# Attention and two feed-forward layers on one core: pinned first splits, four bias buffers, later loads and a new order of the attention stage

## The chip, the core and the metric

The kernel runs on one core of one Trainium2 chip. TensorE (PE) multiplies matrices from SBUF into PSUM, VectorE (DVE) and ScalarE (ACT) work elementwise and read PSUM, GpSimd (POOL) works elementwise on SBUF alone, and SyncE (SP) issues nearly all DMAs, each in its own queue and in order. The metric is device time in microseconds (us); lower is better.

## The reference

```
scores = q @ k.T / sqrt(D)                       # B=2, H=8, S=576, D=64
x      = log1p(|i - j|) / log1p(max(i, 1))
bias   = relu(x * w1 + b1) @ w2                  # hidden width 32, one value for each head
attn   = softmax(scores + bias);  y = attn @ v   # then tokens x 512
out1   = sum_e p[:, e] * (relu(y @ W1[e]) @ W2[e])        # 4 experts, 512 -> 1024 -> 512
h      = out1 @ w_in;   P = a0+a1*h+a2*h^2+a3*h^3;   Q = 1+|b0||h|+|b1|h^2
out    = (P / (Q + 1e-6)) @ w_out                # 512 -> 2048 -> 512
```

All of it is float32. Where a product runs in the faster float32r form, its operand is split into a high part and a remainder, and the two parts are multiplied apart.

## The kernel before

Three stages follow each other: attention, which ends at about 197 us of the span, the expert layer, and the second feed-forward layer. The change touches only the attention stage.

**The bias.** The 576 x 576 bias of the eight heads is made in 36 groups `gg` of 16 query rows. For each group four tiles `hid` are made (`hidden`, L443 on ACT or L445 on DVE: one add and one relu over 288 to 576 columns, SBUF to SBUF), the PE multiplies them by a 32-column weight into one bank (`products`, L460), and one engine scales the bank into a row buffer `bo` (`combine`, L477 on ACT or L479 on DVE: two instructions for the first 32 groups, one for the last four). Each filled row of `bo` is stored to DRAM (`store`, L466), and after eight groups a chunk of bias for the first pair of heads is read back (`load_bias`, L543). There are two buffers `bo` of four rows each, in the pool slots that weights use later.

**One pass of attention.** Eight passes `n` take two heads each. Raw `q`, `k`, `v` are loaded (`load_raw`); `q` and `k` are split into a high part (`split_hi`, L584 on ACT, L586 on POOL) and a remainder (`split_lo`, L592 on POOL or DVE), transposed by the PE (`qk_T`, L608) and copied out on ACT (L616); `kl` is a copy of `kh` with its halves swapped, made by two DMAs (L621, L622). Nine groups `g` of 128 rows of scores follow (`scores`, L651). For each, DVE adds the bias and finds the row's extreme (`biased`, L665), ACT takes the exponential (`exps`, L673), DVE makes the reciprocal of the sums (L679, L684), DVE or POOL scales the rows (`norm`, L694), the PE transposes them (`transp`, L711; `transp_rest`, L724 and L727), and ACT or DVE copies them out (`copies`, L737 and L739). Twice a pass `av` multiplies them by the values: one matmul of all 128 value columns for the tile `pe` that the two heads share (L750), then four pairs of 64-column matmuls, one for each head (L753).

**What sets the order.** Nothing loops in this order in the program. `attention` gives every step as an operation with an engine, a duration, a list of steps that it needs and an urgency; `Flow.emit` plays these operations through, one engine each, and issues them in the order of the starts that come out. `PICK` says which engine takes each step that several could do, `CFG` holds the urgencies, `LAG`, `START` and `ARRIVES` the assumed delays. On the chip each engine then works its queue strictly in that order, and waits on semaphores. The planner lets steps of POOL and some of DVE (`PORT`: the tiles `hid`, `norm`, `split_lo`) not overlap; nothing in the built program enforces this. `TURN` is what the planner charges the PE for a change between array shapes of 32, 64 and 128 columns.

Of the kernel before, what the change touches and what calls it, by code (L numbers as in the profile page):

```python
# [9 lines left out]
F32 = mybir.dt.float32  # L10
# [14 lines left out]
P = 128  # L25
# [3 lines left out]
def f32_of_bits(b):  # L29
# [15 lines left out]
START = dict(PE=7.0, ACT=6.0, DVE=5.9, POOL=6.0, SP=7.5)  # L45
ARRIVES = dict(k=7.5, q=8.5, v=12.0, ident=6.5, ltab=10.0)
# [3 lines left out]
PICK = dict(hid="DDDDADAAADADDDADDADDAADDDDAAADDADDADDAADADDDDDDADDDDDDDDADDDDDADDDDDADDA"  # L50
              "DADADDDADDADDDADADDDAADADADDDDDDADDDADDADADDADDDADDAADDDDDDDADAAAADDDDDD",
            comb="AADDAAADDAADAAADADDAAADAAAADAAAAADDD",
            norm="DPDDPPDPPDPDDDPPDPDDDPDPDPPPPPPDPDPPDDDPDDPDPDDPPPDPPPPDPPPDDDPDDPPDPDPD",
            copy="ADADAADAAADDDAADDADDADDADADAADADAADAADDDADDAAAAADADADAADADDAAADDAADADDAA",
            rest="AAAAAAAADAAADAAAAAAAADAAAAAAAADAAAAAAAADAAAADAAAAAAADAAAAAAAADDAAADAAADD",
            high="PPAPAAPAPAAAAPPP",
            low="PPPDPPPDPDDPPPDP")

LAG = {"PE": .2, "ACT": .16, "DVE": .17, "POOL": .14, "SP": 4.2, "": 0.0, "own": .1, "ownPE": 0.0}
CFG = dict(S=(727.25, 1885.1, -835.03, -1091.88), R=(-435.51, -579.68, 887.76, 715.99),  # L60
           E=(2212.38, 3581.84, 2714.22, 1346.79), A=(-3009.34, -17.34, -2741.04, 809.11),
           N=(-1089.85, -18.23, -1346.32, 1155.82), T=(-970.49, -103.24, -1026.56, -1581.52),
           H=(-626.93, 112.8, -71.3, -1255.47), L=(1318.56, -792.88, -3831.2, -2180.55),
           V=(1383.81, 1813.71, 2683.79, -2574.27), G=(-1937.23, -222.49, -2871.65, -240.27),
           X=(-271.21, -1565.23, -1071.66, 1882.08), sk=(2779.05, -696.25, 887.14, 2612.94),
           sq=(-733.34, 2450.48, 615.97, 34.95), sv=(108.87, 720.22, 1146.45, -407.83),
           qk=(-1735.11, 1178.98, -1793.42, 1880.39), qq=(-2386.03, 493.54, -2804.99, -1502.57),
           kl=(-555.07, -2633.95, 1999.51, 3316.56), b=(1465.24, -1009.62, -3395.64, 567.95), NPB=5, EPS=0.0,
           w0=58, w1=24, w2=56, rk=(2354.82, 1606.83, 519.78, 448.01), rq=(678.94, -1446.52, 1914.62, -188.04),
           rv=(1641.63, 2113.44, -124.18, -2095.68), st=-137.14, F=1386.21,  # L70
           b0=(-2989.02, -989.69, -701.83, -1532.45, -694.41), b1=(659.94, -3385.72, 1251.53, -536.4, 233.82),
           b2=(-3325.06, -1303.49, -2104.11, -2246.44, -1403.66),
           b3=(-3088.15, -311.99, 937.07, 2166.6, 909.33), b4=(-2727.97, -2702.25, -1351.83, 1603.0, -344.56))


class Flow:
    def __init__(self, eps, **busy):
        self.ops, self.free, self.caps, self.eps = [], {"": 0.0, "port": 0.0, **busy}, {}, eps
        self.mode = 128
# [33 lines left out]
    def emit(self):  # L113
# [7 lines left out]
        while ready:  # L121
# [6 lines left out]
            start, _, _, o = min((c for c in cand if first[c[3]["eng"]] == now and c[0] <= now + self.eps), key=lambda c: c[1:3])  # L128
# [30 lines left out]
class Kernel:  # L159
    def __init__(self, ctx, tc, t):  # L160
        self.ctx, self.tc, self.nc, self.t = ctx, tc, tc.nc, t


# [236 lines left out]
    def bias_setup(self):  # L400
# [17 lines left out]
        self.load_raw(0, "v")  # L418
# [19 lines left out]
        def hidden(gg, q, e):  # L438
            tt = 4 * gg + q
            ht = hid[gg, q] = hids[:, tt % 12, 0:width(gg)]  # L440
            d, c = dtab[:, 0:width(gg)] if gg < NM else ltab[:, 572 - 4 * tt:572 - 4 * tt + S], shift[:, tt:tt + 1]
            if e == "ACT":
                nc.scalar.activation(out=ht, in_=d, func=AF.Relu, bias=c)  # L443
            else:
                nc.vector.tensor_scalar(out=ht, in0=d, scalar1=c, scalar2=0.0, op0=ALU.add, op1=ALU.max)  # L445
# [25 lines left out]
        def combine(gg, e):  # L471
# [8 lines left out]
            if G == 0:  # L480
                outs[b] = self.wpool.tile([P, 4, S + MARGIN * (gg < NM)], F32, tag="we", bufs=2, name="bo")
# [13 lines left out]
        def bias_ops(fl, biasop):  # L495
# [3 lines left out]
            for gg in range(NG):  # L499
# [6 lines left out]
                if gg % 4 == 0:  # L506
                    bo = fl.hold("bo", 2)
                co = fl.pick("comb", gg, {"ACT": .8 if gg < NM else .75, "DVE": .87 if gg < NM else .7}, u("b2"), lambda e, gg=gg: combine(gg, e), [po, co], take=[bo] if gg % 4 == 0 else [], free=[ph])
                stored.append(co if gg >= NM else fl.op("SP", .5, u("b3"), lambda gg=gg: store(gg), [co], free=[bo] if gg % 4 == 3 else []))
                if gg % 8 == 7:  # L510
                    biasop[0, c] = fl.op("SP", .6, u("b4"), lambda c=c: self.load_bias(0, c), stored)
                    stored = []
            biasop[0, 4] = fl.op("SP", 1.5, u("b4"), first_last_bias, stored)
# [66 lines left out]
    def split_hi(self, n, nm, e):  # L580
        nc, raw = self.nc, self.raw[n, nm]
        s = self.front.tile([P, 9, 2, D], F32R, tag="spl" + nm, bufs=1, name="spl" + nm)
        if e == "ACT":
            nc.scalar.activation(out=s[:, :, 0, :], in_=raw, func=AF.Copy)  # L584
        else:
            nc.gpsimd.tensor_scalar(out=s[:, :, 0, :], in0=raw, scalar1=1.0, scalar2=1.0, op0=ALU.mult, op1=ALU.mult)  # L586
        self.spl[n, nm] = s

    def split_lo(self, n, nm, e):
        raw, s = self.raw.pop((n, nm)), self.spl[n, nm]  # L590
        eng = self.nc.vector if e == "DVE" else self.nc.gpsimd
        eng.tensor_tensor(out=s[:, :, 1, :], in0=raw, in1=s[:, :, 0, :].bitcast(F32), op=ALU.subtract)  # L592
# [32 lines left out]
    def attention(self):  # L625
# [120 lines left out]
        def av(n, half):  # L746
# [37 lines left out]
        def schedule():  # L784
# [5 lines left out]
            fl = Flow(cfg["EPS"], **START)  # L790
# [6 lines left out]
            a = fl.op("SP", 4.0, 40, self.load_const)  # L797
# [5 lines left out]
            for nm in "kqv":  # L803
                raw_op[0, nm] = fl.op("", ARRIVES[nm], 0, lambda: None)

            def prepare(n):
# [6 lines left out]
                for nm in "kqv":  # L813
                    deps = avop[n - 1] if nm == "v" else [split_op[n, nm]]
                    raw_op[n + 1, nm] = fl.op("SP", .6 if nm == "k" else 1.64, g + 9 + off("r" + nm, n), lambda n=n, nm=nm: self.load_raw(n + 1, nm), deps + [qk_ops[n, "k"][-1] if nm != "k" and n else None])
# [13 lines left out]
                    if nm == "k":  # L829
                        done.append(fl.op("SP", 1.0, g + off("kl", n), lambda n=n: self.swap_k(n), done))  # L830
# [3 lines left out]
            for n in range(8):  # L834
                p_hold = {}
                for r in range(9):
# [32 lines left out]
                    if n % 2 and (h == 1 or last) and n < 7:  # L869
                        biasop[n // 2 + 1, c] = fl.op("SP", 1.5 if last else .6, g + off("b", n), lambda n=n, c=c: self.load_bias(n // 2 + 1, c), [Rop[g], last_store if last else None])  # L870
                    if r in (3, 8):
# [3 lines left out]
                        vo = fl.op("PE", (2.3, 2.84)[half], g + off("V", n), lambda n=n, half=half: av(n, half), deps, take=[one], free=[pt_hold[n, half]], mode=(128, 64))  # L875
# [5 lines left out]
            w = [fl.op("SP", 3.0, cfg["w0"], lambda: (self.stage_w(), self.stage_w()), [Rop[cfg["w0"] - 2]])]  # L881
# [440 lines left out]
```

## Time and profile before

| | us |
|---|---|
| median of 3 runs (788.11 to 790.86) | 788.57 |
| the profiled execution, its own time | 789.93 |
| its span, first to last instruction | 788.1 |
| PE busy | 764.8 (97%) |
| DVE, ACT, POOL busy | 634.3, 464.0, 379.9 |
| PE busy in the first 64 us | 49.44 |

The profile gives, for one execution, the busy time of each engine, a chain of waits that is followed back from the last instruction, and a timeline. A timeline row has the start, the time from the first start to the last end of a merged group, the engine, the line, what is written from what, the shape and the count; in brackets stands how long the engine sat idle before and what ended that. The spans of neighbouring instructions on one engine overlap a little, so that a cost is best read from start to start.

### The profile page before, as it was taken

Reading aid. Unit: us, or ns where it says so; the run is one execution under the profiler, and the core shown is the slowest. Engines: PE = TensorE matmul, PEld = TensorE weight load, DVE = VectorE, ACT = ScalarE, POOL = GpSimd, SP = SyncE. Lnnn points to the kernel's source line nnn. Section 1 sums busy time; section 2 is a strip of 40 time slices with the busy share of each in tenths; the row PEclk is TensorE's granted clock in tenths of the full one; section 3 lists DMA queues with packets and bytes.
Section 4 is the critical chain, followed back from the end, with each engine's and each line's share of the span. In section 5 each row is a group of like instructions: output and inputs, shape, how many; then the busy total and the mean of one; then the engine's idle time right before and its main releaser. Section 6 shows DMA issues by size and latency. Waiting matters only on the chain.

```text
span 788.1 us, 12955 instructions
## 1 busy us (share of the span) xinstructions
PE 764.8 (97%) x4724; PEld 657.4 (83%) x4724; DVE 634.3 (80%) x1168; ACT 464.0 (59%) x894; POOL 379.9 (48%) x362
## 2 busy tenths in 40 slices
PE   6789999999999999999999999999999999999997
PEld 3337878877989988999998899999888889899986
DVE  7998978878679888898888788887677667887875
ACT  7899878875334333234333334333279998887772
POOL 3203434351285543564544465543258977755442
PEclk9999999999999999999999999999999999999999
DMA  6987956751014433444433444432121311000012
GB/s 168 314 279 204 230 142 148 197 139 30 28 54 138 140 104 115 134 149 128 136 99 106 146 140 135 127 110 78 55 81 54 107 54 54 1 0 1 1 41 80
DMA packets 70448, 87.62 MB, mean 111 GB/s; under 512 B 34288, under 2 KB 42736, under 8 KB 70256
## 3 DMA queue, kind: packets, MB, share of 16 engines
q1 hardware_dynamic: 69808, 86.63, 37.4%
q8 instruction: 37, 0.61, 0.3%
q10 hardware_dynamic: 576, 0.16, 0.1%
q14 instruction: 27, 0.22, 0.1%
HBM read 60.15 MB, written 21.61 MB: 104 GB/s over the span
## 4 chain that ended last, share of the span: by engine, by line
PE 76%; DVE 7%; POOL 5%; issue 4%; ACT 3%; DMA 3%; SPq 0%; POOLq 0%; DVEq 0%; ACTq 0%
PE ps_o L926 20%; PE ps_y L1018 10%; PE ps_o L1184 10%; PE ps_h L1176 9%; PE ps_x L1018 8%; PE ps L651 5%; PE ps L753 4%; PE ps L711 4%; DVE hid L445 3%; POOL we L325 2%; DMA bias_d<-bo 2%; PE ps_x L916 1%; PE ps L608 1%; DMA wstg<-w_d 1%; PE ps L460 1%
## 5 line engine op out<-in xcount | busy, mean ns | idle before, releaser
L926 PE MATMUL ps_o<-we,hs 128*128 128x512 f32 x810 | 203.4, 392 | 0.0
L926 PEld LDWEIGHTS ps_o<-we,hs 128*128 128x128 f32 x810 | 146.0, 188 | 25.9
L932 DVE SCALAR_TENSOR_TENSOR acc<-ps_o,prob,acc 128x512 f32<-128x512 f32 x135 | 99.7, 743 | 29.4 <-PE ps_o L926 29.3
L325 POOL TENSOR_TENSOR we<-wstg,we 128x512 fp32r<-128x512 f32 x40 | 57.4, 1455 | 129.7 <-ACT we L319 129.7
L1184 PE MATMUL ps_o<-wmh,hs 128*128 128x512 f32 x252 | 83.5, 392 | 1.0 <-POOL hs L1168 1.0
L1157 POOL TENSOR_TENSOR qq<-qq,ha 128x384 f32<-128x384 f32 x48 | 48.9, 1019 | 71.2 <-ACT qq L1154 69.4
L1176 PE MATMUL ps_h<-x,wmh 128*128 128x384 f32 x288 | 73.7, 336 | 0.0
L956 ACT ACTIVATE hs<-ps_x 128x576 fp32r<-128x576 f32 x32 | 20.8, 651 | 82.5 <-DVE ps_x L1030 75.6
L694 POOL TENSOR_SCALAR P<-P,ri 128x576 f32<-128x576 f32 x38 | 31.0, 821 | 74.6 <-DVE ri L684 24.2
L673 ACT ACTIVATE P<-P,nm 128x576 f32<-128x576 f32 x72 | 55.5, 775 | 10.1 <-DVE nm L665 9.3
L665 DVE CUSTOM_DVE_ANT_0 P<-ps,bias 128x576 f32<-128x576 f32 x72 | 53.2, 751 | 5.3 <-PE ps L651 2.9
L1163 DVE SCALAR_TENSOR_TENSOR qq<-qq,rr 128x384 f32<-128x384 f32 x48 | 26.6, 554 | 38.0 <-ACT rr L1162 38.0
L1184 PEld LDWEIGHTS ps_o<-wmh,hs 128*128 128x128 f32 x252 | 47.3, 188 | 11.3 <-POOL hs L1168 1.9
L460 PE MATMUL ps<-hid,wm 128*32 128x288 f32 (+18 forms) x352 | 41.7, 523 | 14.1 <-DVE hid L445 7.8
L1176 PEld LDWEIGHTS ps_h<-x,wmh 128*128 128x128 f32 x288 | 52.6, 188 | 2.0
L350 POOL TENSOR_TENSOR wu<-wt,wu 128x512 fp32r<-128x512 f32 x28 | 36.2, 1312 | 36.6 <-ACT wu L346 36.6
L1168 POOL TENSOR_TENSOR hs<-pp,hs 128x384 fp32r<-128x384 f32 x48 | 49.0, 1020 | 3.2 <-issue 2.8
L651 PE MATMUL ps<-kh,qs 128*128 128x288 f32 x168 | 49.6, 317 | 0.6 <-DVE nm L665 0.6
L1184 PE MATMUL ps_o<-wml,hs 128*128 128x512 f32 x126 | 49.5, 393 | 0.0
L1018 PEld LDWEIGHTS ps_y<-x,wu 128*128 128x128 f32 x336 | 47.5, 188 | 2.2
L1018 PEld LDWEIGHTS ps_x<-sums,wu 128*128 128x128 f32 x336 | 47.5, 188 | 2.2
L1018 PEld LDWEIGHTS ps_y<-sums,wu 128*128 128x128 f32 x336 | 47.5, 188 | 2.2
(144 smaller groups left out, 1878.7 us busy)
## 6 DMA issues: line engine op xcount, KB each, us to landing
wstg<-moe_w SPq DMA_DIRECT2D x32, 512.0 KB, 4.0
bias_d<-bo SPq DMA_DIRECT2D x32, 295.5 KB, 4.4
bias<-bias_d SPq DMA_DIRECT2D x16, 576.0 KB, 5.5
w<-moe_w_in SPq DMA_DIRECT2D x16, 512.0 KB, 4.5
w<-moe_w_out SPq DMA_DIRECT2D x16, 512.0 KB, 4.0
kl<-kh SPq DMA_DIRECT2D x16, 288.0 KB, 4.8
w_u<-wmag SPq DMA_DIRECT2D x16, 256.0 KB, 2.5
w_d<-wmag SPq DMA_DIRECT2D x16, 256.0 KB, 2.4
```

Source lines behind the costliest of these rows:

```text
L325: nc.gpsimd.tensor_tensor(out=lo[:, sl], in0=stg[:, sl], in1=hi[:, sl].bitcast(F32), op=ALU.subtract)
L460: nc.tensor.matmul(to[32 * q:32 * q + 32, 0:b - a], lhsT=wm, rhs=hs[q][:, a:b], start=True, stop=True)
L651: nc.tensor.matmul(ps[:, half, dst:dst + w], lhsT=lhs, rhs=k[:, src:src + w], start=(i == 0), stop=(i == len(m) - 1))
L665: nc.vector.tensor_tensor_reduce(out=Pt[u][:, S * h:S * h + S].rearrange("p (a b) -> p a b", a=2), in0=ps[:, :, 0:288], in1=self.bias_t[n ...
L673: nc.scalar.activation(out=pt, in_=pt, func=AF.Exp, scale=-1.0, bias=stat.pop(g), accum_out=sums[n, c][:, h:h + 1])
L926: nc.tensor.matmul(ps, lhsT=a, rhs=w[:, f, :], start=(f == i == 0), stop=(f == 1 and i == 2))
L932: nc.vector.scalar_tensor_tensor(out=acc[:, t], in0=ps, scalar=pr, in1=acc[:, t], op0=ALU.mult, op1=ALU.add)
L1018: nc.tensor.matmul(ps[:, half, 0:288], lhsT=wu[:, w, i, k], rhs=x[v][:, k, 288 * half:288 * half + 288], start=(start and k == j == 0), st ...
L1157: nc.gpsimd.tensor_tensor(out=qq, in0=qq, in1=ha, op=ALU.mult)
L1168: nc.gpsimd.tensor_tensor(out=lo, in0=pp, in1=hi.bitcast(F32), op=ALU.subtract)
L1176: nc.tensor.matmul(ps, lhsT=w[:, k, fo:fo + P], rhs=x2_rows(q, v, k), start=(k == i == 0), stop=(k == 3 and i == 2))
L1184: nc.tensor.matmul(ps, lhsT=a[:, P * tt:P * tt + P], rhs=w[:, f % 2, :], start=(f == i == 0), stop=(f == 3 and i == 2))
```

## The change

- **The order searched anew.** `PICK`, `CFG`, and the planner's durations and delays of DMAs are other numbers. A new term `M` (`stay`) makes the planner put off a step that changes the PE's array shape. Of the 144 `hid` tiles DVE makes 89 (99 before); of the 36 combines 19 (13 before); of the 72 copies 23 (33 before); of the 16 high splits POOL makes 11 (8 before); of the 72 `norm` steps POOL makes 40 (38 before).
- **`behind`.** Splits on POOL of passes 0 and 1 get a semaphore wait on the `hid` tile of DVE that the plan has last ahead of them.
- **Four `bo` buffers.** Every second group of four rows now takes a slot of the pool `att` (tag `pt1`).
- **Later loads.** The values of pass 0 are loaded after group 16, `k` of pass 1 after group 16, its `q` and `v` after group 24, the constants of the later layers after the last group.
- **Column halves.** `av` multiplies the shared tile by each head's 64 value columns apart, into that head's half of the bank, and does so last and not first.

```diff
-            start, _, _, o = min((c for c in cand if first[c[3]["eng"]] == now and c[0] <= now + self.eps), key=lambda c: c[1:3])
+            start, _, _, o = min((c for c in cand if first[c[3]["eng"]] == now and c[0] <= now + self.eps), key=lambda c: (c[1] + self.stay * (self.turn(c[3]) > 0), c[2]))
...
+        ahead = None
         for _, _, o in sorted(started, key=lambda x: x[:2]):
-            o["fn"]()
+            ins = o["fn"]()
+            if o["alts"]:
+                kind, i, _ = o["alts"]
+                if o["eng"] == "POOL" and kind in ("high", "low") and i < 4 and ahead is not None:
+                    self.behind(ins, ahead)
+                if o["eng"] == "DVE" and kind == "hid":
+                    ahead = ins
...
+    def behind(self, ins, ahead):
+        ins, ahead = (getattr(x, "ins", x) for x in (ins, ahead))
+        self.tc.add_manual_dep(ins, ahead.name, mybir.DependencyInfo(mybir.DependencyClass.Sync, mybir.DependencyReason.DATA), reason="order")
...
-        self.load_raw(0, "v")
...
-                outs[b] = self.wpool.tile([P, 4, S + MARGIN * (gg < NM)], F32, tag="we", bufs=2, name="bo")
+                pool, tag = (self.wpool, "we") if b % 2 == 0 else (self.att, "pt1")
+                outs[b] = pool.tile([P, 4, S + MARGIN * (gg < NM)], F32, tag=tag, bufs=2, name="bo")
...
-            nc.tensor.matmul(ps[:, :W], lhsT=vs[:, 4:6].rearrange("p h d -> p (h d)"), rhs=shared[:, :W], start=True, stop=False, skip_group_check=True)
-            for e in range(4):
+            for e in range(5):
                 for h in range(2):
-                    nc.tensor.matmul(ps[64 * h:64 * h + 64, :W], lhsT=vs[:, 6 * h + e], rhs=main[:, e, h, :W],
-                                     start=False, stop=(e == 3), skip_group_check=True)
+                    nc.tensor.matmul(ps[64 * h:64 * h + 64, :W], lhsT=vs[:, 6 * h + e] if e < 4 else vs[:, 4 + h], rhs=main[:, e, h, :W] if e < 4 else shared[:, :W],
+                                     start=(e == 0), stop=(e == 4), skip_group_check=True)
...
-            a = fl.op("SP", 4.0, 40, self.load_const)
+            a = fl.op("SP", 4.0, 40, self.load_const, [made[NG - 1]])
...
+            raw_op[0, "v"] = fl.op("SP", 1.7, -1, lambda: self.load_raw(0, "v"), [made[16]])
```

POOL at the start of the program, before. `splq` and `splk` are the splits of `q` and `k` (first the high part, then the remainder), `wm` the bias weight, `qs` the transposed queries, `P` the exponentials:

```order
L564 MEMSET rawv 64x64 x4
L424 ISA
L424 TENSOR_TENSOR wm<-cw,mask 128x32
L586 TENSOR_SCALAR splq<-rawq 128x9x64
L592 TENSOR_TENSOR splq<-rawq,splq 128x9x64
L586 TENSOR_SCALAR splk<-rawk 128x9x64
L592 TENSOR_TENSOR splk<-rawk,splk 128x9x64
L602 MEMSET qs 128x64
```

POOL at the same place, after:

```order
L437 TENSOR_TENSOR wm<-cw,mask 128x32
L600 TENSOR_SCALAR splk<-rawk 128x9x64
L605 TENSOR_TENSOR splq<-rawq,splq 128x9x64
L615 MEMSET qs 128x64
L578 MEMSET rawv 64x64 x4
L600 TENSOR_SCALAR splk<-rawk 128x9x64
L707 TENSOR_SCALAR P<-P,ri 128x576
L605 TENSOR_TENSOR splk<-rawk,splk 128x9x64
L707 TENSOR_SCALAR P<-P,ri 128x576 x3
```

Four splits of pass 0 stood on POOL in a row; two are left there (the others are on DVE and ACT), and the splits of `k` for pass 1 now have a `norm` of the scores between them.

DVE at the start, before (`hid` tiles, then the first combines into `bo`):

```order
L445 TENSOR_SCALAR hid<-dtab,shift 128x576 x4
L445 TENSOR_SCALAR hid<-dtab,shift 128x560
L445 TENSOR_SCALAR hid<-dtab,shift 128x544 x2
L445 TENSOR_SCALAR hid<-dtab,shift 128x528 x3
L445 TENSOR_SCALAR hid<-dtab,shift 128x512 x3
L479 TENSOR_SCALAR bo<-ps,rpsi 128x47
L479 TENSOR_SCALAR bo<-ps,rpsi 128x544
```

DVE at the start, after:

```order
L458 TENSOR_SCALAR hid<-dtab,shift 128x576 x3
L458 TENSOR_SCALAR hid<-dtab,shift 128x560 x3
L458 TENSOR_SCALAR hid<-dtab,shift 128x544
L492 TENSOR_SCALAR bo<-ps,rpsi 128x15
L492 TENSOR_SCALAR bo<-ps,rpsi 128x576
L458 TENSOR_SCALAR hid<-dtab,shift 128x544
L458 TENSOR_SCALAR hid<-dtab,shift 128x528 x2
```

A combine now stands behind the seventh `hid`, the one that POOL's first split waits for.

PE at the end of the bias groups, before (`hid,wm` are the last bias groups, `kh,qs` and `kl,qs` scores, `splk` and `splq` transposes of `k` and `q`; shown with buffer numbers):

```order
L651 MATMUL ps_697<-kl_443,qs_343 128x288
L460 MATMUL ps_707<-hid_110,wm_151 32x288 x8
L460 MATMUL ps_724<-hid_110,wm_151 32x288 x8
L460 MATMUL ps_737<-hid_110,wm_151 32x288 x8
L608 MATMUL ps_750<-identr_141,splq_440 128x128 x3
```

PE at the same place, after (`ident,P` are transposes of scaled scores):

```order
L621 MATMUL ps_708<-identr_131,splk_672 128x128 x3
L724 MATMUL ps_715<-ident_77,P_467 128x128 x4
L621 MATMUL ps_724<-identr_131,splk_672 128x128 x3
L621 MATMUL ps_728<-identr_131,splk_672 128x128 x3
L473 MATMUL ps_734<-hid_110,wm_141 32x288 x8
L724 MATMUL ps_758<-ident_77,P_554 128x128 x4
L473 MATMUL ps_766<-hid_110,wm_141 32x288 x8
L473 MATMUL ps_781<-hid_110,wm_141 32x288 x8
L724 MATMUL ps_797<-ident_77,P_554 128x128 x4
```

The last three bias groups came in one block before the first transpose of scores; now three transposes of scores and the splits of the next `k` stand before or between them.

## Rows read from the trace of the kernel before

**Rows 1.** Busy time by stretch; first row names the columns, x counts instructions.
```profile
core 0: us, PE busy (x) PEld busy (x) DVE busy (x) ACT busy (x) POOL busy (x), PEclk, DMA share, GB/s
0.00:64.00 64.00, 49.44 (x416) 23.21 (x417) 57.19 (x149) 54.22 (x114) 13.83 (x19) 0.97 0.80 244
64.00:197.00 133.00, 130.97 (x1040) 108.29 (x1039) 110.33 (x344) 105.34 (x254) 52.78 (x68) 1.00 0.61 157
```
**Rows 2.** Timeline of DVE, 0 to 64 us: start, length, line, tile, count, idle before.
```profile
5.06 3.06 DVE L445 TENSOR_SCALAR hid<-dtab,shift 128x576 f32<-128x576 f32 x7
8.89 5.10 DVE L445 TENSOR_SCALAR hid<-dtab,shift 128x528 f32<-128x528 f32 x6 [0.78 <-PE ps L460]
13.91 1.81 DVE L479 TENSOR_SCALAR bo<-ps,rpsi 128x47 f32<-128x47 f32 x4
...
26.33 4.91 DVE L445 TENSOR_SCALAR hid<-dtab,shift 128x368 f32<-128x368 f32 x16
...
34.08 0.96 DVE L479 TENSOR_SCALAR bo<-ps,rpsi 128x287 f32<-128x287 f32 x2 [0.79 <-DMA bias_d<-bo]
...
36.71 0.96 DVE L479 TENSOR_SCALAR bo<-ps,rpsi 128x303 f32<-128x303 f32 x2 [1.07 <-PE ps L460]
...
40.82 0.75 DVE L665 CUSTOM_DVE_ANT_0 P<-ps,bias 128x576 f32<-128x576 f32 x1
...
56.99 1.80 DVE L445 TENSOR_SCALAR hid<-ltab,shift 128x576 f32<-128x576 f32 x4
58.71 0.74 DVE L665 CUSTOM_DVE_ANT_0 P<-ps,bias 128x576 f32<-128x576 f32 x1
```
**Rows 3.** Timeline of DVE, 33 to 45 us, whose last group is cut there.
```profile
42.81 2.35 DVE L445 TENSOR_SCALAR hid<-dtab,shift 128x416 f32<-128x416 f32 x3
```
**Rows 4.** Timeline of POOL: the splits from 8 to 45 us.
```profile
8.73 1.41 POOL L592 TENSOR_TENSOR splq<-rawq,splq 128x576 fp32r<-128x576 f32 x1
10.11 0.85 POOL L586 TENSOR_SCALAR splk<-rawk 128x576 fp32r<-128x576 f32 x1
11.04 1.47 POOL L592 TENSOR_TENSOR splk<-rawk,splk 128x576 fp32r<-128x576 f32 x1
...
26.65 5.11 POOL L586 TENSOR_SCALAR splq<-rawq 128x576 fp32r<-128x576 f32 x1 [13.76 <-PE ps L608]
43.06 1.44 POOL L592 TENSOR_TENSOR splk<-rawk,splk 128x576 fp32r<-128x576 f32 x1 [11.29 <-ACT splk L584]
```
**Rows 5.** Timeline of PE: the step behind the last bias group, scores behind `av`.
```profile
61.69 0.46 PE L608 MATMUL ps<-identr,splq 128*128 128x128 f32 x3
...
69.41 0.40 PE L651 MATMUL ps<-kh,qs 128*128 128x288 f32 x1
69.65 0.29 PE L651 MATMUL ps<-kl,qs 128*128 128x288 f32 x1
69.77 0.29 PE L651 MATMUL ps<-kh,qs 128*128 128x288 f32 x1
```
**Rows 6.** Chain of waits, in order of time: start, length, what.
```profile
27.03 6.92 DMA bias_d<-bo
...
64.83 1.06 PE ps L711 x8
...
66.11 1.06 PE ps L651 x8
67.17 0.43 PE ps L750 x2
67.60 1.88 PE ps L753 x16
...
78.41 2.30 PE ps L753 x16
```
**Rows 7.** DMA issues of the page: count, KB each, median us from issue to landing.
```profile
bias_d<-bo SPq DMA_DIRECT2D x32, 295.5 KB, 4.4
bias<-bias_d SPq DMA_DIRECT2D x16, 576.0 KB, 5.5
```

More of the change, by code (lines that the diff above doesn't have):

```diff
@@ L44 @@
 MARGIN = 15
-START = dict(PE=7.0, ACT=6.0, DVE=5.9, POOL=6.0, SP=7.5)
-ARRIVES = dict(k=7.5, q=8.5, v=12.0, ident=6.5, ltab=10.0)
+START = dict(PE=6.0, ACT=5.06, DVE=5.06, POOL=6.0, SP=7.5)
+ARRIVES = dict(k=7.5, q=8.5, ident=6.5, ltab=10.0)
 PORT = {("DVE", "hid"), ("DVE", "norm"), ("DVE", "low")}
@@ L49 @@
 NAMES = dict(D="DVE", A="ACT", P="POOL")
[L50 to L73, printed above, removed]
@@ new lines @@
+PICK = dict(hid="ADDDDDDAAADDADADADDDDAADADADDDDDDAAADADDDDAAADDDDDDDDDAADDDAADAADDDDADDA"
+              "ADADDDAADDADDDADDAADDADADADDADDADAAAADDADDADAADADADAADDDDADADDDDDDDDADDA",
+            comb="DAADAADADDDAADDDADAAADADDDADADDADAAD",
+            norm="PPDDPPPPDPPDDDPPDPDPPDPDPPPPDPPDDDDPPDDPPDPDDPPDDPPDDPPDDDPPDPPDPDDPPPPD",
+            copy="ADDADDAADDAADAADAAAAAADAADADADADADAAADAAAAAAAADDAADADDAAAAAAAAAADAADADAA",
+            rest="AAADAAAAAAAADAAADAAAADAAAAAAAAAAAADAAAAAAAAADAAADAAAAAAAADAAADAAAADAAADD",
+            high="PAPAPPAAPPAPPPPP",
+            low="DPPDPPPPDDPPDPPP")
@@ L76, with __init__ @@
 class Flow:
-    def __init__(self, eps, **busy):
+    def __init__(self, eps, stay, behind, **busy):
         self.ops, self.free, self.caps, self.eps = [], {"": 0.0, "port": 0.0, **busy}, {}, eps
+        self.stay, self.behind = stay, behind
         self.mode = 128
@@ L444, in hidden @@
             else:
-                nc.vector.tensor_scalar(out=ht, in0=d, scalar1=c, scalar2=0.0, op0=ALU.add, op1=ALU.max)
+                return nc.vector.tensor_scalar(out=ht, in0=d, scalar1=c, scalar2=0.0, op0=ALU.add, op1=ALU.max)
         def products(gg):
@@ L581, in split_hi @@
         nc, raw = self.nc, self.raw[n, nm]
-        s = self.front.tile([P, 9, 2, D], F32R, tag="spl" + nm, bufs=1, name="spl" + nm)
+        s = self.spl[n, nm] = self.front.tile([P, 9, 2, D], F32R, tag="spl" + nm, bufs=1, name="spl" + nm)
         if e == "ACT":
@@ L788, in off @@
                 return cfg[kind][min(n, 2) + (n == 7)]
-            fl = Flow(cfg["EPS"], **START)
+            fl = Flow(cfg["EPS"], cfg["M"], self.behind, **START)
             Top, Sop, Rop, Lop, Lop2, split_op, qk_ops, stk = ({} for _ in range(8))
@@ L829, in prepare @@
                     if nm == "k":
-                        done.append(fl.op("SP", 1.0, g + off("kl", n), lambda n=n: self.swap_k(n), done))
+                        done.append(fl.op("SP", 1.2, g + off("kl", n), lambda n=n: self.swap_k(n), done))
                     qk_ops[n, nm] = done
@@ L874, in schedule @@
                         one = fl.hold("one", 4)
-                        vo = fl.op("PE", (2.3, 2.84)[half], g + off("V", n), lambda n=n, half=half: av(n, half), deps, take=[one], free=[pt_hold[n, half]], mode=(128, 64))
+                        vo = fl.op("PE", (2.15, 2.69)[half], g + off("V", n), lambda n=n, half=half: av(n, half), deps, take=[one], free=[pt_hold[n, half]], mode=(64, 64))
                         avop.setdefault(n, []).append(vo)
```

38 lines of the change are left out of this document (27 added, 11 removed).

## The prediction

> **What bounds the kernel now.** I read the busy time by stretch first [rows 1]. After 64 us the PE is the limit: it works 130.97 of the next 133 us, and idles 2.0. In the first 64 us it works only 49.44, while DVE works 57.19 and ACT 54.22: there the making of the bias feeds the PE, and DVE is the fuller of the two feeders. So the change can win only what the PE idles before 64 us (14.6, of which 5.1 pass before DVE's first `hid`), the 2.0 behind, and what it saves in PE work.
>
> Next comes DVE's timeline [rows 2, 3], read for time that is not work. Tiles in an undisturbed run take 4.91/16 = 0.31 us at 331 columns on average, and 3.06/7 = 0.44 at 565, so 0.41 at 520. The six tiles from 8.89 to 13.91 should take 2.5 and took 5.0: 2.6 lost, while POOL ran three splits of 1.41, 0.85 and 1.47 [rows 4]. The three tiles at 42.81 should take 1.1 and took 2.35, beside a POOL split of 1.44: 1.2 lost. DVE also idled 0.78 and 1.07 for the PE and 0.79 for a store of `bo`; that store's leg of the chain of waits is 6.92 long [rows 6]. Together DVE loses 6.4 us before its last `hid` ends at 58.7.
>
> **The change part by part.** *Fewer and pinned splits.* The pass 0 split of `k` (0.85) now follows DVE's seventh `hid`, behind which DVE combines, reading PSUM: no loss. The remainder of `k` moves to DVE. POOL's remainder of `q` (1.41) is released by a `hid` with two combines behind it, 1.8 us [rows 2]: no loss. The pass 1 split of `k` waits for the second far `hid`, behind which DVE has small work, a bias add and a combine: no loss. Its remainder (1.41) follows on POOL behind a `norm` and ahead of another, each priced as a high split, 0.85, the same form and size. These 3.1 us meet a run of three far tiles; I charge 0.4, between nothing and 3.1. What is queued behind the pinned split on POOL is the first `norm`, and the PE's first transpose of scores waits for that.
>
> This rests on how DVE and POOL share SBUF. A split that arrived inside a run of 16 tiles took 5.11 and cost the run nothing (0.31 a tile); three that began before DVE's tiles cost DVE 2.6 [rows 2, 4]. The Trainium skill, SBUF — State Buffer, section Who interferes with whom, says that whichever of the two issues first holds the shared pair for its whole instruction and the other fully blocks. The 2.6 agrees; the 5.11 does not, since the split waited for many tiles. By the rule alone a split waits for one tile at most, and the second rival below would be right, 790.1.
>
> *Idle of DVE that stays.* I followed the new order row by row with these durations. The first combine waits 0.6 for the PE (0.78 before). Two combines in the middle wait 0.3 and 0.8 for groups whose ACT tiles come late. One bias add waits 1.1, as its scores stand on the PE behind the first transpose, which waits for POOL. With four `bo` buffers the 0.79 goes: group 16 then waits for stores of groups 0 to 3. With the 0.4 of port, 3.2 lost. I take 1.2 as the least (the first wait, and half of the two in the middle) and the old 6.4 as the most.
>
> *More work on DVE.* By the order, DVE has before its last `hid`: 7.5 more combines at 0.9, +6.8; 77 near tiles of 32,800 columns against 88 of 37,104, -3.7; one far tile more, +0.45 (1.80/4); two bias adds more at 0.7, +1.4 [rows 2]; two `norm` at 0.45, the far tile's form, +0.9; six tiny steps, +0.5 as an estimate between 0 and 1; the remainder of `k`, +0.7 (nearest is the bias add, 0.74; POOL's 1.41 is the upper end). Sum +7.0. ACT is relieved of as many combines and takes ten tiles, so it isn't late.
>
> *The end of the bias groups.* DVE's last `hid` then ends at 58.7 + 7.0 - (6.4 - 3.2) = 62.5, and the PE, which needs 0.6 for the group that it completes, is done at 63.1 instead of 61.7 [rows 5]. But it has then done more: one scores step (0.53), three transposes of scores (0.53 each) and two thirds of a transposing of `k` (0.5 in all) [rows 5, 6], together 2.6. Gain: 61.7 + 2.6 - 63.1 = 1.2. Behind that two more transposes stand ahead of the first `av`; they wait for a copy out of PSUM (0.7 as a bias add), three tiny steps and POOL's `norm` (0.85), while the PE has 0.75 left to do: 1.1 idle where there was 0.2, so -0.9.
>
> *Fewer changes of array shape.* In the attention stage the order has 13 steps from 128 to 64 columns and 12 back (15 and 15 before), and two fewer to and from 32. Going in costs 0.17: pairs of `av` cost 0.42/4 for each 64 columns (2.30 against 1.88), so four pairs of 256 take 1.71 of the 1.88 [rows 6]. Coming back costs 0.11: the first scores matmul takes 0.24 to the next, the second 0.12 [rows 5]. Saved: 2 x 0.17 + 3 x 0.11 + 2 x 0.1 = 0.9.
>
> *Column halves.* The shared matmul takes 0.43 for 256 columns; a pair of halves takes 4 x 0.42/4 = 0.42 by the same difference: nothing. The cover is that two halves run side by side.
>
> *Later loads.* 21 small loads move behind 8 to 36 stores on SP. What they cover is needed much later, so they cost nothing on their own. But the load of `k` for pass 2 waits on SP for POOL's pinned remainder (about 57.2 by my walk), and behind it stand the last store of the last full chunk and that chunk's load: 57.2 + 4.4 + 5.5 [rows 7] is 67.1; the bias add that needs it comes at about 69. It costs nothing with 2 us to spare.
>
> *The rest of the stage.* Ten copies go from DVE to ACT, seven steps to POOL. DVE (83% in 64 to 197 us) and ACT (79%) change places, POOL stays under half [rows 1]. I leave the 2.0 idle as it is, between 1.0 and 4.0.
>
> Sum: 1.2 - 0.9 + 0.9 = 1.2 us. The profiled execution took 789.93, 1.8 beyond its span and 1.4 above the median; the sum is a difference in the span, so I take it from the median: 788.57 - 1.2 = 787.4.
>
> **The rivals.** *All cover holds* (faster): DVE loses only 1.2 and the late transposes don't wait. 1.2 + 2.0 + 0.9 = 4.1: 784.5, and 783.5 if the later idle halves too. For it: the three pinned splits each meet PSUM work. Against it: DVE's work grows by 7.0 whatever happens to its port.
>
> *POOL takes its time from DVE*: as at 8.89, the 3.1 us near the last tiles are charged whole and not 0.4, so 2.7: 790.1. This is how the page named above has it.
>
> *The pinned split starves* (slower): if the pass 1 remainder meets the run of far tiles as the split at 26.65 met its run, it takes 5.11 - 0.85 = 4.3 longer, and the transposes of `k`, which stand in order on the PE ahead of the last bias groups, move all behind them: 791.7. It decides when DVE reaches the run before POOL has the port. Against it: the run is three tiles, then tiny steps.
>
> *Halves one after the other* (slower): if two column halves that read one moving tile don't run side by side, 8 x 0.43 + 8 x 0.53 = 7.7 more: 795.1. Against it: the pairs of heads do, in the row of 1.88.
>
> **How the numbers follow.** Forecast 0.46, full cover 0.25, POOL from DVE 0.14, starving 0.10, halves 0.05. The likeliest is 787.4. The range takes in full cover with the later idle halved, 783.5, and starving, 791.7; halves are left out, as is the worst of all bounds together (DVE losing all of 6.4 and the later idle doubled, 793.5). A measurement of this kernel tells about 0.5% from no change, 3.9 us: faster means under 784.6, which only full cover gives, 0.25; slower means over 792.5, halves and half of starving, 0.10; the rest, 0.65, is no change.
>
> **What would show it.** In the changed profile: six early tiles at 0.41 each and no POOL split over 1.5 us beside them; the first bias add near 34 us (40.82 before [rows 2]); DVE's last far tile at about 62.5 and the PE's last bias group at about 63.1; the shared matmul at 0.43 for each 256-column `av`; PE idle of 64 to 197 us near 2. If the first bias add is at 34 but the PE's busy time in the first 64 us hasn't grown, the extra DVE work ate the gain. If the PE's waits name POOL's split of `k` with over 2 us, it starved. If the idle behind 64 us has grown past 4, the new order and not the bias stage decides, and the forecast is wrong for that reason.

## The result, and the profile after

The changed kernel takes 796.47 us (median of four runs, 793.99 to 796.66) where the kernel before took 789.35 beside it: the ratio is 1.0082, interval 1.0054 to 1.011. It is slower, by about 7 us. The forecast was 787.4 with a range of 783.5 to 791.7, so the time lies outside, on the side to which it gave 0.10. The profiled execution took 796.66, its span 794.9; that of before was 788.1.

Busy time by stretch, changed kernel (columns as in [rows 1], whose two rows these answer):

```profile
0.00:64.00 64.00, 52.38 (x425) 24.86 (x425) 57.50 (x156) 56.57 (x115) 8.48 (x19) 1.00 0.81 247
64.00:197.00 133.00, 125.86 (x1010) 106.78 (x1010) 99.85 (x321) 103.48 (x255) 55.97 (x71) 0.96 0.61 155
```

The first stretch did what the change says: the PE works 52.38 us of the first 64, 2.9 more than before. The second lost it and more: 125.86 of 133 instead of 130.97, so its idle grew from 2.0 to 7.1, and the granted clock fell to 0.96. What the PE waited for, up to 210 us (engine, line, waited for: total, times, longest):

```profile
PE ps L664 <- DMA kl<-kh: 6.8, 2, 5.0
PE ps L473 <- ACT hid L456: 6.7, 3, 6.0
```

The second row is the start of the kernel, as before. The first is new: twice the scores stood before `kl`, which two DMAs on SP (the swap) make for each pass. The kernel before had no such row. The chain of waits of the changed kernel goes through both places (start, length, what); first pass 2:

```profile
77.61 9.17 DMA kl<-kh
...
88.89 0.72 PE ps L621 x6
89.61 1.09 PE ps L664 x4
90.70 0.85 PE ps L724 x4
```

then pass 7:

```profile
164.71 0.52 ACT kh L629
...
168.49 6.73 DMA kl<-kh
...
175.36 2.02 PE ps L664 x7
177.38 1.71 PE ps L724 x8
179.09 1.81 PE ps L664 x8
180.90 0.87 PE ps L724 x8
181.77 1.05 PE ps L664 x8
```

Read the last five rows of pass 7 together: eight scores matmuls take 1.05 and eight transposes 0.87 at full clock, but behind the gap 2.02 (seven), 1.71 and 1.81. That is 5.54 for work of 2.84: 2.7 us lost to the half clock on top of a wait of 4.95. Behind the first gap the last three rows, 2.66 in all, stand for some 1.6: 1.1 lost. So the late stretch lost 5.1 of idle and 3.8 of clock, the first gained 2.9: 6.0 of the 6.8 us between the two spans. This count is rough. It leaves out that the kernel before had a stretch at half clock of its own in the first 64 us (granted 0.97 there [rows 1], 0.50 from 36 to 38 us), which the changed kernel did not have; by some 3.4 us at half clock, an estimate from that trace, that is up to 1.7 us more gained, and so much more of the 6.8 without a place. The experiments below tell better what the two places are worth.

Why was the swap of pass 7 late? Its last input, `kh`, was written at 165.23, but SP issued it at 167.95. SP's queue in the changed kernel (start, length, line, what, count):

```profile
154.17 13.69 SPq L306 DMA_DIRECT2D wstg<-moe_w  x3
167.95 0.50 SPq L634 DMA_DIRECT2D kl<-kh  x1
```

and in the kernel before:

```profile
158.65 1.14 SPq L292 DMA_DIRECT2D wstg<-moe_w  x2
163.74 0.49 SPq L621 DMA_DIRECT2D kl<-kh  x1
...
173.11 0.37 SPq L292 DMA_DIRECT2D wstg<-moe_w  x1
```

`wstg` is a staging buffer, two in number, for the expert weights of the next stage, 512 KB a load. Before, two loads stood ahead of the swap and the third behind it. Now the third stands ahead, and it must wait until POOL (the step on the weights behind ACT's, L339) has let go of a buffer, which is the last of SP's waits for it:

```profile
SPq L306 <- POOL we L339: 2.6, 1, 2.6
```

SP stands with the third load for some 12 us (the row of 13.69, of which the first two took about 1.1), and the swap stands behind. What the load brings is first read at 210.9.

And the swap of pass 2? It was issued in time (77.06 and 77.61) but its second half landed 9.17 later. What DMA did just ahead (share in the last column but one), changed kernel and then before:

```profile
68.00:72.00 4.00, 3.86 (x34) 3.73 (x34) 3.06 (x10) 3.26 (x8) 0.00 (x0) 1.00 0.20 11
...
80.00:84.00 4.00, 4.00 (x37) 3.47 (x34) 2.99 (x10) 3.98 (x11) 1.61 (x2) 1.00 1.08 327
```

```profile
68.00:72.00 4.00, 4.00 (x36) 3.31 (x33) 2.79 (x12) 2.59 (x8) 3.37 (x4) 1.00 0.98 336
```

From 68 to 72 the DMA engines moved 11 GB/s, and 336 before. SP was issuing the small loads for the experts' shares, of 1 to 8 KB, which the change had put there:

```profile
65.69 0.63 SPq L240 DMA_DIRECT2D ab<-moe_a  x1
66.36 0.43 SPq L241 DMA_DIRECT2D ab<-moe_b  x1
66.83 3.95 SPq L243 DMA_DIRECT2D dp<-moe_domain_probs  x6
```

Behind them the loads of `q`, the 1152 KB store of the last chunk, bias loads and the swap came all at once.

### The profile page after: what moved, and what is told of

Its sections match the earlier page's. It is cut to its first block, busy times and chain, and to the rows that moved or that the text cites. A ratio compares the mean times of both kernels' runs of the same rounds, so it can differ in the third digit from the quotient of the medians.

```text
span 794.9 us, 13031 instructions
## 1 busy us (share of the span) xinstructions
PE 769.3 (97%) x4756; PEld 662.5 (83%) x4756; DVE 625.6 (79%) x1159; ACT 466.6 (59%) x900; POOL 377.4 (47%) x365
## 4 chain that ended last, share of the span: by engine, by line
PE 75%; ACT 6%; POOL 5%; issue 4%; DVE 4%; DMA 4%; SPq 1%; DVEq 0%; POOLq 0%; ACTq 0%
PE ps_o L939 20%; PE ps_y L1031 10%; PE ps_o L1197 10%; PE ps_h L1189 9%; PE ps_x L1031 8%; PE ps L664 5%; PE ps L765 4%; PE ps L724 4%; DMA kl<-kh 2%; POOL we L339 2%; ACT hid L456 1%; POOL wml L339 1%; PE ps_x L929 1%; PE ps L473 1%; PE ps L621 1%
## 5 line engine op out<-in xcount | busy, mean ns | idle before, releaser
L339 POOL TENSOR_TENSOR we<-wstg,we 128x512 fp32r<-128x512 f32 x40 | 57.0, 1448 | 137.1 <-ACT we L333 137.1
L664 PE MATMUL ps<-kl,qs 128*128 128x288 f32 x168 | 46.8, 303 | 6.8 <-DMA kl<-kh 6.8
L664 PE MATMUL ps<-kh,qs 128*128 128x288 f32 x168 | 51.5, 327 | 0.3 <-DVE nm L678 0.2
```

What stands on the lines that cost most here:

```text
L339: nc.gpsimd.tensor_tensor(out=lo[:, sl], in0=stg[:, sl], in1=hi[:, sl].bitcast(F32), op=ALU.subtract)
L664: nc.tensor.matmul(ps[:, half, dst:dst + w], lhsT=lhs, rhs=k[:, src:src + w], start=(i == 0), stop=(i == len(m) - 1))
```

## The experiments

All but three edits are moves in the finished order: the planner runs as it did, and then a named step is put behind another one, so nothing else moves. The runs f2, f3 and f4 change the lines shown and keep the order; g4 adds the lines of the pin. Times are medians over five rounds (5 to 12 executions); a ratio is to the kernel before on the same chip. In the later edits each pair of `MOVES` puts the steps with the first name behind the step with the second.

| run | edit | time | ratio | interval |
|---|---|---|---|---|
| e1_weights | changed kernel, third weight load behind the swap of pass 7 | 790.23 | 1.0007 | 0.9995 to 1.002 |
| e2_const | changed kernel, small loads later | 794.71 | 1.0056 | 1.0043 to 1.007 |
| e3_bias | changed kernel, one bias load behind the swap of pass 2 | 797.37 | 1.0094 | 1.0081 to 1.0106 |
| e4_all | the three edits | 786.30 | 0.9958 | 0.9945 to 0.9971 |
| g5_two | e1 and e2 | 786.32 | 0.9954 | 0.9937 to 0.997 |
| g1_before_late_swap | kernel before, swap of pass 7 behind the third weight load | 799.17 | 1.0119 | 1.0102 to 1.0136 |
| g4_before_pin | kernel before, pin alone | 788.48 | 0.9986 | 0.9975 to 0.9997 |
| f2_no_pin | e4 without the pin | 786.63 | 0.9958 | 0.9946 to 0.997 |
| f3_two_bo | e4 with two `bo` buffers | 787.75 | 0.9975 | 0.9966 to 0.9984 |
| f4_whole | e4 with the shared tile whole | 787.44 | 0.9967 | 0.9956 to 0.9979 |
| f1_early_k | e4 with `k` of pass 1 loaded earlier | 785.98 | 0.9942 | 0.993 to 0.9954 |
| g3_free_k1 | f1 with the pin on pass 0 alone | 785.81 | 0.9949 | 0.9932 to 0.9967 |

**The third weight load.** It is issued at the end of POOL's step; the edit holds it until the swap of pass 7 is out.

```diff
         def low():
...
-            self.stage_w()
+            if (7, "kl") in self.stk:
+                self.stage_w()
+            else:
+                self.held += 1
...
         self.stk[n, "kl"] = sw
+        if n == 7:
+            for _ in range(self.held):
+                self.stage_w()
```

> The changed kernel with one edit: the third load of expert weights stands on SP behind the swap of k for pass 7 and not ahead of it. Theory (SP's order): the swap then goes out when the last copy of kh ends (165.2 in the changed kernel's trace) and not at 167.95, lands near 170.9, and the scores wait about 0.7 us and not 4.95; the stretch at half clock behind that wait (about 2.3 us lost from 175.4 to 180.7) goes too or mostly. Time 790.5, between 789 and 792; PE idle of 64 to 197 us about 3. Rival (the order as a whole is too tight there: the last copy of kh itself stands behind a conversion of weights on ACT, so the scores find another late input): the wait falls to 3 at best and the half clock stays, time 794 to 796.

790.23, in the middle of what the theory expected. SP's queue, and the PE's stretch from 160 to 182 us, which in the changed kernel had 17.05 of 22 at clock 0.84:

```profile
154.66 1.14 SPq L306 DMA_DIRECT2D wstg<-moe_w  x2
166.08 0.50 SPq L637 DMA_DIRECT2D kl<-kh  x1
...
168.30 0.37 SPq L306 DMA_DIRECT2D wstg<-moe_w  x1
```

```profile
160.00:182.00 22.00, 22.00 (x177) 17.96 (x176) 17.65 (x59) 19.92 (x48) 9.43 (x11) 1.00 0.34 91
```

No wait and no half clock are left in that stretch. The rival (the last copy of `kh` is itself too late) falls. The load ahead had cost twice: it held the swap's issue (167.95 against `kh` at 165.23, 2.7 us), and the swap then landed in 5.9 to 6.7 us beside 512 KB, against 3.3 to 4.1 in this run.

**The reverse, in the kernel before.** The same order made in the other kernel:

```diff
+MOVES = [(("kl", 7), "weights")]
...
+        for what, behind in MOVES:
+            some = [o for o in order if o.get("tag") == what]
+            order = [o for o in order if o.get("tag") != what]
+            at = next(i for i, o in enumerate(order) if o.get("tag") == behind) + 1
+            order[at:at] = some
```

> The kernel before with one edit, the reverse of the first experiment: its swap of k for pass 7 stands on SP behind the third load of expert weights, as in the changed kernel. There that load waits for POOL's second step on the weights, which ended at 173.1, and the first scores of pass 7 stood at 172.3. Theory (one load ahead of a swap on an in-order queue is what the changed kernel lost): the swap lands near 178.5 to 179.5, the scores wait 6 to 7 us, and the stretch behind runs at half clock for some 2 us more: 789.4 + 8 = 796 to 799. Rival (the order of the kernel before has slack at this place, other work is drawn forward): under 2 us, 791 at most.

799.17, ten slower than the kernel before, at the upper end of what the theory gave. SP's queue, then the PE behind the gap:

```profile
158.17 14.08 SPq L300 DMA_DIRECT2D wstg<-moe_w  x3
172.29 0.49 SPq L629 DMA_DIRECT2D kl<-kh  x1
```

```profile
180.21 0.58 PE L659 MATMUL ps<-kl,qs 128*128 128x288 f32 x1 [8.71 <-DMA kl<-kh]
```

The same inversion of two lines on SP costs the kernel before 8.71 us of wait and a slow stretch (granted 0.50 from 180 to 184 us), with nothing else of the change in it. The wait is longer than in the changed kernel: there the swap was issued 2.5 us before the scores came to it (167.95 against 170.41), here 0.8 after (172.29 against 171.50). So the cause is the order of these two on SP, not the tightness of the new order.

The Trainium skill, Perfetto Trace Analysis, section DMA Instruction — HWDGE (DVE, Sync), says that the DMA engines do not themselves wait on semaphores; the wait stands in the issuing sequencer. The rows of 13.69 and 14.08 agree: SP issued nothing behind the third load in them until that had gone out.

**The small loads, and a bias load.** Two readings of the late landing at pass 2.

```diff
+MOVES = [("const", ("k", 5)), ("share", ("kl", 5))]
```

> The changed kernel with one edit: the six small loads for the experts' shares (65.7 to 70.8 us on SP) and the five steps that use them stand behind the load of k for pass 5, in a stretch where SP waits anyway. Theory (late small loads): the DMA engines are no longer idle from 68 to 72 us (share 0.20 in the changed kernel, 0.98 before), the loads of q and the store of the last chunk go out 5 us earlier, the swap of k for pass 2 lands in 5 to 6 us and not 9.2, and the PE's wait of 1.84 at 85.1 and the slow stretch behind it (about 1 us) go: time 793.8. Rival (two loads of bias, 576 KB each, stand ahead of that swap where one stood before): the swap still lands after 85.5, time 796 to 797.

```diff
+MOVES = [(("bias", 1, 1), ("kl", 2)),]
```

> The changed kernel with one edit: the second of the two 576 KB loads of bias that stand ahead of the swap of k for pass 2 on SP stands behind it. Rival of the run before (the bias loads delay the swap): the swap lands in 5 to 7 us, the wait of 1.84 is gone, time 793.8. Theory of the late small loads: the stores, loads of q and bias loads are still pushed together, the swap is early by less than 1 us and the bias add that needs the moved load may wait for it, time 796 to 797.

With the small loads out of the way the time is 794.71, 1.8 less than 796.47 where 2.7 was expected; its PE works 27.54 of the 28 us from 72 to 100 (25.95 in the changed kernel, at clock 0.94), and no wait for `kl` at 85 us is left, only that of pass 7:

```profile
PE ps L672 <- DMA kl<-kh: 5.2, 1, 5.2
```

By itself the gain in time is not clear of noise: the interval of this ratio overlaps that of the changed kernel (1.0054 to 1.011).

Moving the bias load did nothing for the time (797.37). It did let the swap of pass 2 land before it was needed, but the loads of `q` behind it then came late, and the PE waited as long one step on:

```profile
94.52 0.62 PE L629 MATMUL ps<-identr,splq 128*128 128x128 f32 x3 [1.92 <-POOL splq L613]
```

So the small loads are the cause of a wait here, and which transfer is last in the queue behind them only decides where the PE waits. That they do it through the DMA time lost from 68 to 72 us is read from the rows and not shown by itself: without them that stretch still had a share of only 0.36 (79 GB/s), and the swap landed in 6.2 to 7.0 us where 5 to 6 was expected, against 8.3 to 9.2 in the changed kernel.

**Both together.**

> The three edits together. If both late swaps are what the time after 64 us lost, the gain of the first stretch comes out: 796.5 - 6 - 2.7 = 787.8, between 786 and 789.5, PE idle of 64 to 197 us about 2 to 3. If the order as a whole is too tight and new waits come up, 791 to 795.

> The changed kernel with the weight load behind the swap and the small loads later, without moving the bias load. The bias load alone did nothing, so the time should be that of the three edits, 786.3 to 787. If the bias load is a part of what the three edits gained over the sum of the single ones (3.9 more than the weight load alone, where the small loads alone gave 1.8), 788 to 788.8.

786.3 both times: 0.9958 and 0.9954 of the kernel before, so the change is a gain of 3 us once two places in SP's queue are put right. The bias load adds nothing. The two edits together give 10.1, 2 more than the single ones add up to; the intervals of the ratios, 1 us either way and 2 for the changed kernel, leave that open. What the small loads cost is better read from e1 to g5, which differ by them alone: 3.9 us, with intervals that don't touch. The PE waits that e1 still had, and g5 has not, are 3.1 of it:

```profile
PE ps L624 <- POOL splq L608: 1.7, 2, 1.2
PE ps L670 <- DMA kl<-kh: 1.4, 1, 1.4
```

PE idle of 64 to 197 us in the run of the three edits is 0.5:

```profile
64.00:197.00 133.00, 132.49 (x1088) 110.52 (x1087) 102.54 (x329) 105.77 (x261) 56.64 (x72) 1.00 0.60 156
```

**The parts of the change, each taken away or put alone.** These four stand on the version of the three edits, or on the kernel before.

```diff
-                if o["eng"] == "POOL" and kind in ("high", "low") and i < 4 and ahead is not None:
+                if o["eng"] == "POOL" and kind in ("high", "low") and i < 0 and ahead is not None:
```

> The three edits, without the waits of the first four GpSimd splits on a VectorE tile. Theory of the forecast (POOL's splits that begin before DVE's tiles take DVE's time): the split of k for pass 0 meets DVE's first tiles again, as in the kernel before, where six tiles took 5.0 and not 2.5; the remainder of q too; the first stretch loses 1 to 3 us: 787.3 to 789.3. Rival (DVE's first tiles aren't on the path, or the splits stand where DVE reads PSUM by the new order alone): 786.3, within 0.6.

786.63, the rival's number: the pin is worth nothing measurable there. POOL's first split and DVE's first tiles without it, and the tiles with it:

```profile
5.89 0.90 POOL L612 TENSOR_SCALAR splk<-rawk 128x576 fp32r<-128x576 f32 x1 [0.92 <-DMA rawk<-k]
```

```profile
4.88 3.46 DVE L469 TENSOR_SCALAR hid<-dtab,shift 128x576 f32<-128x576 f32 x7
8.48 0.96 DVE L503 TENSOR_SCALAR bo<-ps,rpsi 128x15 f32<-128x15 f32 x2
```

```profile
4.89 3.05 DVE L469 TENSOR_SCALAR hid<-dtab,shift 128x576 f32<-128x576 f32 x7
8.49 0.96 DVE L503 TENSOR_SCALAR bo<-ps,rpsi 128x15 f32<-128x15 f32 x2 [0.55 <-PE ps L484]
```

The split does take 0.41 of DVE's time (3.46 against 3.05), but with the pin DVE waits 0.55 for the PE right behind, so both start the combine at the same time. The other pinned step of pass 0, POOL's remainder of `q`, took 2.54 without its pin, beside a run of eleven tiles, where it takes 1.41 with it; the eleven tiles took 3.55 in both runs, so here POOL paid and not DVE:

```profile
25.94 2.54 POOL L617 TENSOR_TENSOR splq<-rawq,splq 128x576 fp32r<-128x576 f32 x1 [19.15 <-ACT splq L610]
```

> The kernel before with the pin alone: its first GpSimd splits wait for the VectorE tile that stands ahead of them in the order. Theory of the forecast (DVE gets back what the splits took, 2.6 us early and 1.2 at 42.8): 1 to 3 us faster, 786.5 to 788.5. Rival (the pin is worth something only where the order puts a combine behind the tile, and here tiles follow): within 0.8 of before, and the split of q at 8 us still runs beside tiles that take over 0.6 each.

Here the pin is put into the kernel before, by the same lines as in the change. 788.48, ratio 0.9986: at most 2 us, about 1. This is the sharpest test of the forecast's arithmetic, for DVE did get its time back. DVE in this run:

```profile
9.40 2.49 DVE L457 TENSOR_SCALAR hid<-dtab,shift 128x528 f32<-128x528 f32 x6 [0.78 <-PE ps L472]
...
21.49 0.96 DVE L491 TENSOR_SCALAR bo<-ps,rpsi 128x143 f32<-128x143 f32 x2 [1.36 <-DMA bias_d<-bo]
...
29.42 2.42 DVE L457 TENSOR_SCALAR hid<-dtab,shift 128x320 f32<-128x320 f32 x8 [0.64 <-PE ps L472]
...
34.93 0.96 DVE L491 TENSOR_SCALAR bo<-ps,rpsi 128x287 f32<-128x287 f32 x2 [1.02 <-DMA bias_d<-bo]
```

The six tiles take 2.49 and not 5.10 [rows 2], as the forecast had it; then DVE waits for stores of `bo` (1.36 and 1.02, where it was 0.79 once) and for the PE. ACT's waits for these stores grew too, from 2.1 to 3.0. So about half of the 3.2 us that DVE works less in the first 64 us (54.02 against 57.19) went into waits for the stores; that the rest was slack against ACT, which feeds the PE with it, is argued and not shown.

```diff
-                pool, tag = (self.wpool, "we") if b % 2 == 0 else (self.att, "pt1")
+                pool, tag = self.wpool, "we"
```

> The three edits, with two bias row buffers (bo) and not four, the order of every engine the same. Theory of the forecast (the four buffers take away one wait of 0.79 for a store): 786.5 to 787.5, with waits of ACT or DVE for stores of bias rows of 0.5 to 1.5 in sum. Rival (combines are now spread otherwise over DVE and ACT and the order was searched for four, so every block of four groups finds its store unfinished): waits of 3 us and more, 789 or later.

787.75, 1.4 more by the medians, with intervals that overlap a little; just outside what the theory gave and far from the rival's time, though the wait is of the rival's size. DVE's waits for stores in that run:

```profile
DVE bo L503 <- DMA bias_d<-bo: 3.6, 1, 3.6
```

One wait of 3.6, where I had priced the four buffers at 0.79 (and had left out a wait of ACT for the same stores, 2.1 in the kernel before); less than half of it reaches the end.

```diff
-            for e in range(5):
...
+            nc.tensor.matmul(ps[:, :W], lhsT=vs[:, 4:6].rearrange("p h d -> p (h d)"), rhs=shared[:, :W], start=True, stop=False, skip_group_check=True)
+            for e in range(4):
```

> The three edits, with the values' shared tile taken whole (one matmul of 128 columns and 16 of halves for each product with the values) and not in column halves. Forecast: the shared matmul costs 0.42 for 256 columns either way, so 786.3 within 0.8. Rival (the halves save a change of array shape inside each of the 16 products, 0.16 to 0.22 each): 2.5 to 3.5 slower, 789 to 790.

787.44, 1.1 more by the medians, a little outside the 0.8 that was expected, with intervals that overlap: the halves cost nothing and may save a little. The rival (2.5 to 3.5) falls.

**The early load of k, and the pin at pass 1.** In the run of the three edits POOL's split of `k` for pass 1 began when its load landed, at 53.0.

```diff
+MOVES = [..., (("v", 1), ("k", 1)), (("bias", 0, 2), ("k", 1)), (("q", 1), ("k", 1))]
```

> The three edits of the run before (two swaps of k freed), and the load of k for pass 1 ahead of the loads of q and v and of the bias load that stand before it on SP. In the run before, POOL's split of that k began at 53.0, when the load landed, and POOL's norm behind it let the PE wait 2.04 at 52.4 and run at clock 0.57 from 56 to 60. Theory (the late load of k sets that wait, not the pin on a VectorE tile): the load goes out at 42 and lands near 47, the split runs before 50, the wait of 2.04 and the slow stretch go: 786.3 - 2 to 3.3 = 783.0 to 784.3. Rival (the pin or the norm's own input sets it, since DVE and ACT are full until 52): the wait stays above 1, 785.5 to 787.

785.98, no gain that can be told from 786.3. The split began at the same time as before, and waited for something else (a step of DVE behind the pinned tile, which ended at 52.7):

```profile
53.03 0.67 POOL L612 TENSOR_SCALAR splk<-rawk 128x576 fp32r<-128x576 f32 x1 [23.25 <-DVE sm L707]
```

So the rival was right here: the pin sets it. The next run takes the pin from pass 1 (`i < 2` in the line above).

> The kernel with the early load of k for pass 1, and the waits on a VectorE tile for the splits of pass 0 alone, so that the split of k for pass 1 starts when its load has landed. In the run with the early load that split still began at 53.03, now held by the pin. Theory (pin and load end at the same time, so taking one away shows the other): the split runs before 50, POOL's norm at 53.1 instead of 53.68, the PE's wait of 1.76 falls to about 1.1: 785.4, that is 0.6 faster. Rival (without the pin the split meets DVE's run of tiles from 47 to 53 and takes its time): the split takes over 2 us or DVE's tiles lose 0.5 to 1.5, and the time is 786 to 787.5.

```profile
46.39 0.67 POOL L612 TENSOR_SCALAR splk<-rawk 128x576 fp32r<-128x576 f32 x1 [16.82 <-PE ps L484]
53.13 0.74 POOL L722 TENSOR_SCALAR P<-P,ri 128x576 f32<-128x576 f32 x1 [6.08 <-DVE ri L712]
```

The split now runs 6.6 us earlier, beside DVE's tiles, in 0.67 and without harm, and then POOL waits for the `norm`'s own input at 53.1, as the theory said. The PE's wait fell to 1.4. The time, 785.81, is the same within the interval: the expected 0.6 is below what five rounds can show. By that row this place is bound by DVE's steps of the first pass ahead of the `norm` (the bias add among them), not by POOL.

## Why the prediction was wrong

**The step that failed** is the last one, "The rest of the stage": I left the PE's idle behind 64 us at 2.0, between 1.0 and 4.0, and it became 7.1, with 3.8 more at half clock. The forecast named this as the way it would be wrong, yet gave it no rival and no price. Two causes, shown by the runs e1, g1 and g5: the third weight load ahead of the swap (a wait of 4.95 and 2.7 of clock in the rows; 6.2 in the time), and the small loads (1.84 and 1.1 in the rows; 1.8 to 3.9 in the time, by e2 and by g5 against e1). Together they are 10.6 in the rows and 10.1 in the time. The 0.10 that the forecast gave to the slower side stood for rivals that did not come true.

**It could have been read.** SP's order of the two kernels has it in plain rows, before:

```
L292 DMA wstg<-moe_w 128x4x256 x2
L621 DMA kl<-kh 64x1152
L622 DMA kl<-kh 64x1152
L292 DMA wstg<-moe_w 128x2x512
```

and after:

```
L306 DMA wstg<-moe_w 128x4x256 x2
L306 DMA wstg<-moe_w 128x2x512
L634 DMA kl<-kh 64x1152
L635 DMA kl<-kh 64x1152
```

The trace of before tells the price: there the third load went out at 173.11, when POOL let go of its buffer, while the swap had gone at 163.74. I had followed SP's queue only as far as the bias stage. The planner doesn't see it either, by the code: the third load is issued inside POOL's step on the weights and has no operation of its own on SP, so in the plan it holds nothing up. That it is why the search chose this order is argued, not shown.

**"Later loads ... cost nothing"** was the second failed step. I asked when the small loads' data is needed, and not what stands behind them: 5.1 us of issue on SP while the DMA engines ran at a share of 0.20, just where four loads of `q`, a store and bias loads were due. The tight transfer that I did name (`k` for pass 2, with 2 us to spare) was near the place but not the one.

**The bias stage went as followed.** The first bias add stood at 33.86 (34 forecast, 40.82 before [rows 2]), seven early tiles took 2.88, 0.41 each, and the last tiles and the last bias group of the changed kernel:

```profile
60.18 1.37 DVE L458 TENSOR_SCALAR hid<-ltab,shift 128x576 f32<-128x576 f32 x3
```

```profile
60.53 2.34 PE L473 MATMUL ps<-hid,wm 128*32 128x288 f32 x32
```

DVE's last `hid` ended at 61.6 (62.5 forecast) and the PE's last bias group at 62.9 (63.1 forecast; 61.7 before [rows 5]). With the two places put right the whole change gains 3.0 by the medians; the sum had 1.2. One of its terms did not come: the 1.1 us of idle ahead of the first `av` (the PE worked all 8 us from 60 to 68). No run tests the 0.9 for fewer changes of array shape. And the worst of all bounds was added up wrongly: 3.2 and 2.0 on top of 787.4 is 792.6, not 793.5.

**But the reason for it was partly wrong.** The sum gave DVE back 3.2 of 6.4 lost us, most of it for the pin. The pin alone gives about 1 (g4), and without it the new order loses nothing (f2): most of DVE's lost time was slack. What carries the stage is then, by exclusion, the new share of work between DVE and ACT with four `bo` buffers (1.4 by f3); no run isolates the share of work, so that is not shown.

**The rivals.** No starving in the changed kernel: POOL's splits of `k` took 0.67 and its remainders 1.42 in passes 0 and 1, and those of pass 1 also without their pins (g3). POOL taking DVE's time: 0.41 once, without the pin, and covered (f2). The Trainium skill, SBUF — State Buffer, section Who interferes with whom, has the other engine blocked for the whole of an instruction. In f2 the first split grew by 0.23 and DVE's tiles by 0.41, together about one split of 0.67, which agrees. But the remainder that took 2.54 there, 1.13 more, waited for longer than one tile, as the split of 5.11 [rows 4] had, and that split took 5.12 again in g1, which keeps the order of the kernel before. So steps of POOL without a pin did starve beside a run of DVE's tiles at two places, and at a third (0.67 at 46.39, g3) not; with the pins they took 0.67 and 1.41, and f2 shows that this was worth no time. Halves one after the other: no, 0.43 for 256 columns (2.31 for twenty in the chain against 1.88 for sixteen [rows 6]) and f4.

## What to carry to other kernels

A queue that issues in order is a resource like an engine: for every DMA that a change moves, ask what it waits for and what stands behind it, and let no transfer that waits for a buffer to come free stand ahead of one that the bound engine needs soon. Small transfers cost the queue by number, not by size (eight of 1 to 8 KB took SP 5.1 us here, 0.64 each, and a load of 512 KB 0.37 in the row at 168.30 of e1), and what they push back arrives in a heap. Time given back to one of two feeders can be lost again at the buffers that they share: here 3.2 us less work for DVE in the first 64 us gave about 1 (g4).

## What the runs showed of the hardware

A wait of the PE can cost more than itself, and its length alone did not tell whether it did. At the same place near 53 us, waits for POOL of 1.88 (e1), 2.04 (e4), 2.15 (e3), 2.28 (f2) and 2.57 (e2) were followed by a stretch at half speed (granted clock 0.57 to 0.69 in the mean of 56 to 60 us), while waits of 1.76 (f1), 2.08 (f4), 2.13 (g5) and 2.24 (the changed kernel) were not (1.00). The much longer ones, 4.95 and 8.71, were. The wait of 1.84 at 85 us in the changed kernel was (0.57 from 88 to 92), the one of 1.4 at that place in e1 was not (1.00). What else decides no run here separates; each of these is one profiled execution, and the mean clock of the changed kernel's four executions went from 0.993 to 0.997. The rows from 175.36 to 181.77 of the chain above show one such stretch and its end.
